# Moving padding columns between the two halves' exponentials, and reordering the first four steps of a dilated-attention plus gated-convolution kernel

## Chip, cores and metric

The kernel runs on one core of one Trainium2 chip. The metric is the device time of one execution in microseconds (us): the median of three runs. A separate execution is recorded by the hardware profiler; all durations of single instructions come from that one.

The engines of the core are called as in the profile: PE (matrix multiply), PEld (PE's loading of weights, which runs beside its matmuls), DVE (vector engine), ACT (scalar engine), POOL (GpSimd) and SP (the engine that here issues most of the transfers). Each engine works through its own instructions in order.

## What is computed

Windowed attention over 8 batches, 8 heads, 576 positions and head width 64, and then a gated unit over the joined heads (width 512). Heads 0 to 3 ("plain") look at the last 32 positions, heads 4 to 7 ("dilated") at every fourth of the last 128.

```python
scores = scale * np.matmul(q, k.transpose(0, 1, 3, 2))
rel = pos[:, None] - pos[None, :]
mask_plain = (rel >= 0) & (rel < window)                       # window 32, heads 0..3
mask_dil = (rel >= 0) & (rel < window * dilation) & (rel % dilation == 0)   # heads 4..7
attn = softmax(where(mask, scores, -1e9));  x = attn @ v       # heads joined: 512 wide
for k in range(K): gate_pre += conv_w[k] * xp[:, k:k + S, :]   # causal, K = 5
gate = 1 / (1 + exp(-gate_pre))
out = (gate * (x @ w_val)) @ w_out
```

All inputs and the output are float32; the kernel computes in bfloat16 with float32 sums.

## The kernel before

**Steps, groups, halves.** The work on attention is cut into 32 steps (`NP`). Step i takes one batch b = i // 4 and a pair of heads c = i % 4; pairs 0 and 1 are plain, 2 and 3 dilated. Two steps make a group g (four heads of one kind), and loads and transposes are made for groups. Inside a step there are two halves, hf = 0 and 1. For each half:

- `scores` (L383) makes six small matmuls into a PSUM tile `ps_sc`; ACT takes the exponential of them (L407) into a half of the tile `et`.
- `apply_mask` (L410) multiplies that half of `et` with a mask of zeros and ones on DVE (L416).
- `attn_v` (L418) makes six matmuls (L434) with 128 columns of `et` as weights and v as the moving operand, which carries a column of ones, so that the row sums come out too.
- `normalize` (L439) takes the reciprocals (L447) and multiplies (L452), on DVE, into `xn`.

One step later `trans_x` (L456) transposes the result into `xT`. The other half of the work is then `conv` (L485), the gate's convolution as six matmuls with diagonal weights `conv_diag` (L503, gate on ACT at L511), `val` (L514, four matmuls and a product on DVE at L524) and `out_tile` (L530, four matmuls, a copy on ACT at L538 and stores).

**Layout of et.** For plain heads (block width `HB` = 288) the weights of attn_v begin at 96 n in the block of one head (n = 0, 1, 2), for dilated ones at 128 n; the load always takes 128 columns, more than a block has left at n = 2. The four blocks of a step lie side by side, first half then second, with 96 columns of ones behind the last:

```python
ets = [consts.tile([128, 4 * HB + 96], BF16, name=f"et{i}") for i in range(NET)]
e3 = et[:, 2 * hf * HB:2 * (hf + 1) * HB].rearrange("p (h n) -> p h n", h=2)
lhsT=et[:, (2 * hf + sl) * HB + col:(2 * hf + sl) * HB + col + 128],
```

Rows of the product that belong to no position are not read.

**Order.** The schedule is written by hand: every engine's instructions stand in the order in which the Python code issues them, and semaphores between the engines are put in by the framework. Transfers are issued on three queues: SP's (most loads and all stores), ACT's (four loads at the beginning) and POOL's (the two weights `w_val` and `w_out`, cast on the way). `load_main` (L110) loads k or q of two or four heads (L115), `load_rest` (L119) the last positions, `load_v` (L138) v, and `load_group` (L164) all of a group. Groups 0 and 1 are loaded in two parts of two heads, group 2 and later ones whole; group g + 3 is issued at the first step of group g.

`cast` (L171) turns k or q of plain groups into bfloat16: for group 0 on DVE and ACT, for later ones on POOL. `trans_main` (L314) and `trans_rest` (L355) transpose k and q of the next group, with copies on ACT and DVE. `make_conv_diag` (L300) builds the five diagonals of one 128-wide block; block c is built at step c on POOL. `warm` (L568) issues matmuls on a tile of ones whose result nobody reads. `pop_conv` (L564) takes the next conv of a list when its due time, i or i + 0.5, is less than the number given.

Of the kernel before, what the change touches and what calls it, by code (L numbers as in the profile page):

```python
# [23 lines left out]
def kernel(  # L24
# [60 lines left out]
    NET = 2  # L85
    ets = [consts.tile([128, 4 * HB + 96], BF16, name=f"et{i}") for i in range(NET)]
    NVP = 2
# [49 lines left out]

    def load_v(g, a=0, e=4):  # L138
        b, dil = g // 2, g % 2
        t = grp_tiles.setdefault(g, {})  # L140
        if not dil:

            dst = vPs[b % NVP].rearrange("p h n e -> p (h n) e")
            first = a * NB
            if b == 0 and a == 0:
                nc.sync.dma_start(out=dst[32:128, 0, 0:D], in_=v[0, 0, 0:96, :])
                first = 1
            nc.sync.dma_start(
                out=dst[:, first:e * NB, 0:D],
                in_=bass.AP(  # L150
                    tensor=v.tensor, offset=v.offset + (b * H * S + 96 * first - 32) * D,
                    ap=[[D, 128], [96 * D, e * NB - first], [1, D]]))
        else:
            if "vst" not in t:
                t["vst"] = vst_pool.tile([128, 4, DIL * D], FP32, name="v_st")
                t["vBst"] = vst_pool.tile([128, 4, 2, D], FP32, name="vB_st")
            nc.sync.dma_start(
                out=t["vst"][:, a:e, :],
                in_=v[b, 4 + a:4 + e, 0:RM, :].rearrange("h (p r) d -> p h (r d)", r=DIL))
            nc.sync.dma_start(  # L160
                out=t["vBst"][:, a:e].rearrange("p h j d -> p h (j d)"),
                in_=v[b, 4 + a:4 + e, DIL * TB:S, :].rearrange("h (p j) d -> p h (j d)", j=2))
# [39 lines left out]
    load_rest(0, "q", nc.scalar)  # L202
    load_v(0, 0, 2)
    load_main(0, "k", 2, 4, nc.sync)
    load_main(0, "q", 2, 4, nc.scalar)
    load_v(0, 2, 4)
    nc.scalar.dma_start(out=conv_nat, in_=moe_conv_w)
    for a in (0, 2):
# [5 lines left out]
        load_v(1, a, a + 2)  # L214
    load_group(2)
    nc.vector.memset(junk, 1.0)  # L216
# [9 lines left out]
    for et in ets:  # L226
        nc.vector.memset(et[:, 4 * HB:], 1.0)
    for i in range(NVP):
# [71 lines left out]
    def make_conv_diag(c):  # L300
        nc.gpsimd.tensor_tensor(  # L301
            out=conv_diag[:, c, :, :],
# [3 lines left out]

    def load_weights():
        for (dst, src) in ((w_val_b, moe_w_val), (w_out_b, moe_w_out)):
            nc.gpsimd.dma_start(out=dst, in_=src.rearrange("(c p) n -> p c n", p=128))

# [72 lines left out]
    def scores(i, hf):  # L383
# [21 lines left out]
        et = ets[i % NET]  # L405
        e3 = et[:, 2 * hf * HB:2 * (hf + 1) * HB].rearrange("p (h n) -> p h n", h=2)
        nc.scalar.activation(out=e3, in_=ps[:, :, 0:HB], func=AF.Exp, scale=scale)  # L407
        st[(i, "et")] = et

    def apply_mask(i, hf):  # L410
        b, c, dil, g, a = pair_info(i)
        et = st[(i, "et")]
        e3 = et[:, 2 * hf * HB:2 * (hf + 1) * HB].rearrange("p (h n) -> p h n", h=2)
        m = mask_d if dil else mask_p[:, 3 * hf:3 * hf + 3, :].rearrange("p n q -> p (n q)")
# [3 lines left out]
    def attn_v(i, hf):  # L418
        b, c, dil, g, a = pair_info(i)
        et, ps = st[(i, "et")], st[(i, hf)]  # L420
        for n in range(3):
            for sl in range(2):
# [3 lines left out]
                else:  # L426
# [8 lines left out]
                    out=ps[:, 0, x * AVS:x * AVS + D + 1],  # L435
                    lhsT=et[:, (2 * hf + sl) * HB + col:(2 * hf + sl) * HB + col + 128],
                    rhs=rhs, start=True, stop=True)
# [139 lines left out]
    trans_rest(0)  # L577
    cast(0, "k", 2, nc.vector)
    cast(0, "q", 2, nc.scalar)
    setup_conv_w()  # L580
    for i in range(NP):
        b, c, dil, g, a = pair_info(i)
        if c % 2 == 0 and g + 3 < 2 * B:
            load_group(g + 3)
        if i + 1 < NP:
            prep_v(i + 1)
        if i == 0:
            make_mask_d()
            make_perm()
        g2 = g + 2  # L590
        if g2 < 2 * B and g2 % 2 == 0:
            cast(g2, "k" if a == 0 else "q", 0, nc.gpsimd)
            cast(g2, "k" if a == 0 else "q", 2, nc.gpsimd)
        if i < NCH:
            make_conv_diag(i)
        if i == 1:
            load_weights()
        scores(i, 0)
        scores(i, 1)
        if i > 0:  # L600
            trans_x(i - 1)
            for G in range(2):
                convs.append((i + 0.5 * G, (b - (c == 0), (c - 1) % NCH, G)))
            if c == 0:
                vals.extend((b - 1, cc, G) for G in range(2) for cc in range(NCH))
        if i == 0:
            trans_main(0, "k", (1,))
# [6 lines left out]
        elif i == 3:  # L614
            trans_main(2, "k")
            trans_main(2, "q")
        elif g + 1 < 2 * B:
            trans_main(g + 1, "k" if a == 0 else "q")
        apply_mask(i, 0)
        if i < 3:  # L620
            warm(2)
        if vals:
            run_val()
        pop_conv(i)
        apply_mask(i, 1)
        if i < 3:
            warm(2)
        attn_v(i, 0)
        normalize(i, 0)
        pop_conv(i + 0.5)  # L630
        if i < 3:
            warm(2)
        attn_v(i, 1)
        normalize(i, 1)
        if i == 3:
            trans_rest(2)
        elif i > 3 and a == 0 and g + 1 < 2 * B:
            trans_rest(g + 1)
        if i < 3:
            warm(3)  # L640
        if outs:
# [47 lines left out]
```

## Time and profile before

| | us |
|---|---|
| median of 3 runs | 200.55 (200.37 to 200.99) |
| the profiled execution, its own time | 202.34 |
| its span, first to last instruction | 200.6 |
| PE busy | 176.8 (88%) |
| DVE busy | 129.3 (64%) |
| ACT busy | 118.9 (59%) |
| POOL busy | 45.0 (22%) |
| granted clock of PE, mean | 0.977 |
| moved by transfers | 42.29 MB, 211 GB/s |

How to read it: busy time is the time in which an engine executes; the rest of the span it waits or has nothing to do. The page also cuts the span into 40 slices of about 5 us and gives each engine's busy tenths; PEclk is the clock granted to PE, in tenths. A list of waits gives, for an engine and line, who released it, the us in total, the number of times and the longest. A matmul's end is modelled, and matmuls overlap, so PE's busy time is not a measure of work done at full speed. Line numbers are those of the kernel before.

The four k and q transposes of group 0's first pair end at about 6 us; scores of steps 0, 1, 2, 3 and 4 begin at 6.93, 14.63, 26.00, 33.03 and 36.72 us. From there a step takes 4 to 6 us, depending on how many output tiles it has.

### The profile page before, as it was taken

How to read it: one execution, taken by the hardware profiler on the slowest of the kernel's cores; microseconds unless marked ns; L12 is line 12 of the kernel's file. 1: busy time of each engine (PE TensorE's matmuls, PEld its weight loads, DVE VectorE, ACT ScalarE, POOL GpSimd, SP SyncE). 2: the span in 40 equal slices, each digit the busy share in tenths (PEclk: the TensorE clock that was granted, in tenths of full speed). 3: DMA queues.
4: the chain of work that ended last, by engine and by line, in shares of the span. 5: the costliest groups of instructions: out<-in, count | busy, mean ns of one | idle time of the engine just before them, and what ended most of it. 6: DMA issues, size and time to landing. Idle time of an engine off the chain costs nothing.

```text
span 200.6 us, 5261 instructions
## 1 busy us (share of the span) xinstructions
PE 176.8 (88%) x2046; PEld 124.9 (62%) x2071; DVE 129.3 (64%) x342; ACT 118.9 (59%) x211; POOL 45.0 (22%) x91
## 2 busy tenths in 40 slices
PE   6595598889899999999899999998999999989990
PEld 2452355767667776777577776776677767665650
DVE  3254066787757875877767776777677767774530
ACT  3514054866757765776577658666676757654331
POOL 7200991160440080000900350007104000000000
PEclk9999579999999999999999999999999999999997
DMA  6989999999959993779969975969595222111334
GB/s 171 271 249 323 192 323 204 294 242 367 301 152 275 360 267 86 253 252 268 227 168 356 332 147 142 346 209 286 157 279 187 56 76 78 62 52 56 106 105 157
DMA packets 62499, 42.29 MB, mean 211 GB/s; under 512 B 31237, under 2 KB 57861, under 8 KB 62474
## 3 DMA queue, kind: packets, MB, share of 16 engines
q1 hardware_dynamic: 60592, 40.31, 72.0%
q0 software_dynamic: 1056, 1.05, 3.3%
q10 hardware_dynamic: 826, 0.60, 1.0%
q8 instruction: 16, 0.26, 0.5%
q14 instruction: 9, 0.07, 0.1%
HBM read 33.56 MB, written 9.44 MB: 214 GB/s over the span
## 4 chain that ended last, share of the span: by engine, by line
PE 65%; DVE 19%; DMA 5%; SPq 4%; issue 2%; POOL 1%; ACT 0%; ACTq 0%
PE ps_bank L533 15%; PE ps_bank L518 13%; PE ps_bank L503 11%; DVE et L416 9%; DVE y_all L524 6%; PE ps_sc L434 6%; PE ps_sc L404 6%; PE ps_bank L325 5%; DMA k_nat<-in_k_dram 3%; PE ps_bank L464 3%; SPq L115 2%; DMA q_nat<-in_q_dram 2%; DVE xT L479 2%; PE ps_bank L477 2%; PE ps_bank L570 2%
## 5 line engine op out<-in xcount | busy, mean ns | idle before, releaser
L503 PE MATMUL ps_bank<-xT,conv_diag 128*128 128x288 bf16 (+1 forms) x384 | 50.8, 268 | 4.5 <-POOL conv_diag L301 4.5
L511 ACT ACTIVATE gate<-ps_bank 128x288 bf16<-128x288 f32 x64 | 26.5, 417 | 32.2 <-PE ps_bank L503 31.1
L407 ACT ACTIVATE et<-ps_sc 128x576 bf16<-128x576 f32 x64 | 38.2, 649 | 12.0 <-PE ps_sc L404 10.5
L518 PE MATMUL ps_bank<-xT,w_val_b 128*128 128x288 bf16 x256 | 41.5, 286 | 0.2 <-DVE xT L479 0.2
L524 DVE SCALAR_TENSOR_TENSOR y_all<-gate,ps_bank 128x288 bf16<-128x288 bf16 x64 | 28.9, 452 | 16.0 <-PE ps_bank L518 13.7
L503 PEld LDWEIGHTS <-conv_diag 128*128 128x128 bf16 x384 | 32.2, 98 | 10.8 <-POOL conv_diag L301 4.6
L538 ACT ACTIVATE osb<-ps_bank 128x512 f32<-128x512 f32 x36 | 21.5, 597 | 27.1 <-PE ps_bank L533 26.8
L452 DVE TENSOR_TENSOR xn<-ps_sc,rec 96x384 bf16<-96x384 f32 (+1 forms) x64 | 35.5, 555 | 2.2
L533 PE MATMUL ps_bank<-w_out_b,y_all 128*128 128x512 bf16 x120 | 35.4, 380 | 1.3
L434 PEld LDWEIGHTS <-et 128*128 128x128 bf16 x384 | 22.8, 99 | 16.5 <-DVE et L416 12.2
L181 POOL CAST k_b<-k_nat 128x512 bf16<-128x512 f32 x14 | 8.7, 650 | 96.9 <-DMA k_nat<-in_k_dram 69.8
L518 PEld LDWEIGHTS <-w_val_b 128*128 128x128 bf16 x256 | 23.5, 98 | 9.5 <-issue 0.4
L479 DVE COPY xT<-ps_bank 128x576 bf16<-128x576 bf16 x32 | 14.6, 458 | 20.2 <-PE ps_bank L477 13.7
L447 DVE RECIPROCAL rec<-ps_sc 96x6 f32<-96x6 f32 (+1 forms) x64 | 12.4, 194 | 18.4 <-PE ps_sc L434 17.6
L533 PEld LDWEIGHTS <-y_all 128*128 128x128 bf16 x144 | 12.7, 97 | 12.0 <-DVE y_all L524 3.7
L416 DVE TENSOR_TENSOR et<-et,mask_d 128x576 bf16<-128x576 bf16 x32 | 19.2, 604 | 0.0
L434 PE MATMUL ps_sc<-vP,et 128*128 128x65 bf16 x192 | 14.2, 200 | 2.6 <-DVE et L416 0.6
L570 PE MATMUL ps_bank<-junk 128*128 128x512 bf16 x34 | 13.4, 513 | 1.6 <-DVE junk L216 1.5
L416 DVE TENSOR_TENSOR et<-et,mask_p 128x576 bf16<-128x576 bf16 x32 | 14.7, 465 | 0.0
L434 PE MATMUL ps_sc<-vB,et 128*128 128x65 bf16 x64 | 9.7, 195 | 5.4 <-DVE et L416 4.4
L188 POOL CAST vA<-v_st 128x512 bf16<-128x512 f32 x16 | 10.7, 668 | 11.7 <-DMA v_st<-in_v_dram 11.7
L340 ACT COPY kT<-ps_bank 128x1024 bf16<-128x1024 bf16 (+1 forms) x9 | 8.3, 919 | 2.4 <-PE ps_bank L325 2.1
(78 smaller groups left out, 191.1 us busy)
## 6 DMA issues: line engine op xcount, KB each, us to landing
k_nat<-in_k_dram SPq DMA_DIRECT2D x14, 512.0 KB, 5.8
q_nat<-in_q_dram SPq DMA_DIRECT2D x14, 512.0 KB, 6.0
vP<-in_v_dram SPq DMA_DIRECT2D x7, 768.0 KB, 8.1
v_st<-in_v_dram SPq DMA_DIRECT2D x7, 512.0 KB, 5.6
out_dram<-osb SPq DMA_DIRECT2D x8, 256.0 KB, 2.6
vB_st<-in_v_dram SPq DMA_DIRECT2D x7, 256.0 KB, 5.8
out_dram<-osb SPq DMA_DIRECT2D x8, 224.0 KB, 2.5
out_dram<-osb SPq DMA_DIRECT2D x8, 192.0 KB, 2.3
```

The costliest lines, as they stand in the source:

```text
L407: nc.scalar.activation(out=e3, in_=ps[:, :, 0:HB], func=AF.Exp, scale=scale)
L416: nc.vector.tensor_tensor(out=e3, in0=e3, in1=m, op=ALU.mult)
L434: nc.tensor.matmul(out=ps[:, 0, x * AVS:x * AVS + D + 1], lhsT=et[:, (2 * hf + sl) * HB + col:(2 * hf + sl) * HB + col + 128], rhs=rhs, st ...
L452: nc.vector.tensor_tensor(out=dst, in0=av[:, :, 0:D], in1=rec[0:R, :, None].to_broadcast([R, 6, D]), op=ALU.mult)
L479: nc.vector.tensor_copy(xTs[b % NXT][:, c, :, 2:], pr)
L503: nc.tensor.matmul(out=ps[:, o * T:(o + n) * T], lhsT=conv_diag[:, c, K - 1 - m, :], rhs=xt[:, c, r:r + n, off:off + T], start=(idx == 0), ...
L511: nc.scalar.activation(out=gate, in_=ps[:, 0:HB], func=AF.Tanh, scale=0.5)
L518: nc.tensor.matmul(out=ps[:, 0:HB], lhsT=w_val_b[:, mc, c * 128:(c + 1) * 128], rhs=xt[:, mc, 2 * G:2 * G + 2, 2:], start=(mc == 0), stop= ...
L524: nc.vector.scalar_tensor_tensor(out=y_all[:, c, b * S + G * HB:b * S + (G + 1) * HB], in0=gates.pop((b, c, G)), scalar=1.0, in1=ps[:, 0:H ...
L533: nc.tensor.matmul(out=ps, lhsT=y_all[:, c, 128 * n:128 * n + 128], rhs=w_out_b[:, c, :], start=(c == 0), stop=(c == NCH - 1),)
L538: nc.scalar.mul(out=osb, in_=ps, mul=0.5)
L570: nc.tensor.matmul(out=bank(), lhsT=junk[:, 0:128], rhs=junk, start=True, stop=True)
```

## The change

It has two parts.

1. The tile `et` becomes three-dimensional, one row of 576 + 96 columns for each half, with the 96 columns of ones behind each half instead of behind both. Writers and readers address their half by its index.
2. The beginning is put into another order. v's first part and conv_w move to ACT's queue, q's second half to SP's; group 2 is loaded in two parts. `make_conv_diag` moves from POOL to DVE and to other places: block 0 before the loop, block c + 1 at the end of step c. The second halves of group 0's k and q are both cast on ACT, behind the exponentials of step 0. The transposes for the next group in steps 0 to 4 move from the middle of the step to its end. POOL loads w_val at step 1 and w_out at step 3, and casts k and q of group 2 at step 2, behind the preparation of v. In steps 0 to 3 the warm matmuls are 3, 1 and 1 inside a step (3 more at the end of steps 0 to 2), where they were 2, 2 and 2 in steps 0 to 2; and the due times given to `pop_conv` are a quarter later, so that step 1 runs two convs.

```diff
--- before.py
+++ after.py
@@ -83,7 +83,7 @@
     NKT = 2
     kTs = [consts.tile([128, 2, KOFF + S], BF16, name=f"kT{i}") for i in range(NKT)]
     NET = 2
-    ets = [consts.tile([128, 4 * HB + 96], BF16, name=f"et{i}") for i in range(NET)]
+    ets = [consts.tile([128, 2, 2 * HB + 96], BF16, name=f"et{i}") for i in range(NET)]
     NVP = 2
     vPs = [consts.tile([128, 4, NB, VS], FP32, name=f"vP{i}") for i in range(NVP)]
     NVD = 2
@@ -135,7 +135,7 @@
                     tensor=src.tensor, offset=src.offset + ((b * H + 4) * S + RM) * D,
                     ap=[[DIL * D, TR], [S * D, 4], [1, DIL * D]]))
 
-    def load_v(g, a=0, e=4):
+    def load_v(g, a=0, e=4, eng=nc.sync):
         b, dil = g // 2, g % 2
         t = grp_tiles.setdefault(g, {})
         if not dil:
@@ -143,9 +143,9 @@
             dst = vPs[b % NVP].rearrange("p h n e -> p (h n) e")
             first = a * NB
             if b == 0 and a == 0:
-                nc.sync.dma_start(out=dst[32:128, 0, 0:D], in_=v[0, 0, 0:96, :])
+                eng.dma_start(out=dst[32:128, 0, 0:D], in_=v[0, 0, 0:96, :])
                 first = 1
-            nc.sync.dma_start(
+            eng.dma_start(
                 out=dst[:, first:e * NB, 0:D],
                 in_=bass.AP(
                     tensor=v.tensor, offset=v.offset + (b * H * S + 96 * first - 32) * D,
@@ -154,10 +154,10 @@
             if "vst" not in t:
                 t["vst"] = vst_pool.tile([128, 4, DIL * D], FP32, name="v_st")
                 t["vBst"] = vst_pool.tile([128, 4, 2, D], FP32, name="vB_st")
-            nc.sync.dma_start(
+            eng.dma_start(
                 out=t["vst"][:, a:e, :],
                 in_=v[b, 4 + a:4 + e, 0:RM, :].rearrange("h (p r) d -> p h (r d)", r=DIL))
-            nc.sync.dma_start(
+            eng.dma_start(
                 out=t["vBst"][:, a:e].rearrange("p h j d -> p h (j d)"),
                 in_=v[b, 4 + a:4 + e, DIL * TB:S, :].rearrange("h (p j) d -> p h (j d)", j=2))
 
@@ -200,11 +200,11 @@
     load_main(0, "q", 0, 2, nc.scalar)
     load_rest(0, "k", nc.sync)
     load_rest(0, "q", nc.scalar)
-    load_v(0, 0, 2)
+    nc.scalar.dma_start(out=conv_nat, in_=moe_conv_w)
+    load_v(0, 0, 2, nc.scalar)
     load_main(0, "k", 2, 4, nc.sync)
-    load_main(0, "q", 2, 4, nc.scalar)
+    load_main(0, "q", 2, 4, nc.sync)
     load_v(0, 2, 4)
-    nc.scalar.dma_start(out=conv_nat, in_=moe_conv_w)
     for a in (0, 2):
         load_main(1, "k", a, a + 2, nc.sync)
         load_main(1, "q", a, a + 2, nc.sync)
@@ -212,7 +212,13 @@
             load_rest(1, "k", nc.sync)
             load_rest(1, "q", nc.sync)
         load_v(1, a, a + 2)
-    load_group(2)
+    for a in (0, 2):
+        load_main(2, "k", a, a + 2, nc.sync)
+        load_main(2, "q", a, a + 2, nc.sync)
+        if a == 0:
+            load_rest(2, "k", nc.sync)
+            load_rest(2, "q", nc.sync)
+        load_v(2, a, a + 2)
     nc.vector.memset(junk, 1.0)
 
 
@@ -224,7 +230,7 @@
     for kt in kTs:
         nc.vector.memset(kt[:, :, 0:KOFF], 0.0)
     for et in ets:
-        nc.vector.memset(et[:, 4 * HB:], 1.0)
+        nc.vector.memset(et[:, :, 2 * HB:], 1.0)
     for i in range(NVP):
         nc.vector.memset(vPs[i][:, :, :, D:D + 1], 1.0 - 2.0 ** -9)
         if i == 0:
@@ -298,15 +304,14 @@
             out=conv_w_sb, in_=ps[:, 0:NCH * 8].rearrange("p (c e) -> p c e", c=NCH)[:, :, 0:K])
 
     def make_conv_diag(c):
-        nc.gpsimd.tensor_tensor(
+        nc.vector.tensor_tensor(
             out=conv_diag[:, c, :, :],
             in0=ident[:, None, :].to_broadcast([128, K, 128]),
             in1=conv_w_sb[:, c, :, None].to_broadcast([128, K, 128]),
             op=ALU.mult)
 
-    def load_weights():
-        for (dst, src) in ((w_val_b, moe_w_val), (w_out_b, moe_w_out)):
-            nc.gpsimd.dma_start(out=dst, in_=src.rearrange("(c p) n -> p c n", p=128))
+    def load_weight(dst, src):
+        nc.gpsimd.dma_start(out=dst, in_=src.rearrange("(c p) n -> p c n", p=128))
 
 
     st = {}
@@ -403,14 +408,14 @@
                     rhs = t["qB"][p0:p0 + D, a + hf, :, :]
                 nc.tensor.matmul(out=o, lhsT=lhsT, rhs=rhs, start=True, stop=True)
         et = ets[i % NET]
-        e3 = et[:, 2 * hf * HB:2 * (hf + 1) * HB].rearrange("p (h n) -> p h n", h=2)
+        e3 = et[:, hf, 0:2 * HB].rearrange("p (h n) -> p h n", h=2)
         nc.scalar.activation(out=e3, in_=ps[:, :, 0:HB], func=AF.Exp, scale=scale)
         st[(i, "et")] = et
 
     def apply_mask(i, hf):
         b, c, dil, g, a = pair_info(i)
         et = st[(i, "et")]
-        e3 = et[:, 2 * hf * HB:2 * (hf + 1) * HB].rearrange("p (h n) -> p h n", h=2)
+        e3 = et[:, hf, 0:2 * HB].rearrange("p (h n) -> p h n", h=2)
         m = mask_d if dil else mask_p[:, 3 * hf:3 * hf + 3, :].rearrange("p n q -> p (n q)")
         m = m[:, None, :].to_broadcast([128, 2, HB])
         nc.vector.tensor_tensor(out=e3, in0=e3, in1=m, op=ALU.mult)
@@ -433,7 +438,7 @@
                 x = 3 * sl + n if dil else 2 * n + sl
                 nc.tensor.matmul(
                     out=ps[:, 0, x * AVS:x * AVS + D + 1],
-                    lhsT=et[:, (2 * hf + sl) * HB + col:(2 * hf + sl) * HB + col + 128],
+                    lhsT=et[:, hf, sl * HB + col:sl * HB + col + 128],
                     rhs=rhs, start=True, stop=True)
 
     def normalize(i, hf):
@@ -575,34 +580,58 @@
     trans_main(0, "k", (0,))
     trans_main(0, "q", (0,))
     trans_rest(0)
-    cast(0, "k", 2, nc.vector)
-    cast(0, "q", 2, nc.scalar)
     setup_conv_w()
+    make_conv_diag(0)
     for i in range(NP):
         b, c, dil, g, a = pair_info(i)
         if c % 2 == 0 and g + 3 < 2 * B:
             load_group(g + 3)
-        if i + 1 < NP:
-            prep_v(i + 1)
         if i == 0:
             make_mask_d()
             make_perm()
+        if i + 1 < NP:
+            prep_v(i + 1)
+        if i == 1:
+            load_weight(w_val_b, moe_w_val)
+        if i == 3:
+            load_weight(w_out_b, moe_w_out)
+        if i == 2:
+            for name in ("k", "q"):
+                cast(2, name, 0, nc.gpsimd)
+                cast(2, name, 2, nc.gpsimd)
         g2 = g + 2
-        if g2 < 2 * B and g2 % 2 == 0:
+        if 2 < g2 < 2 * B and g2 % 2 == 0:
             cast(g2, "k" if a == 0 else "q", 0, nc.gpsimd)
             cast(g2, "k" if a == 0 else "q", 2, nc.gpsimd)
-        if i < NCH:
-            make_conv_diag(i)
-        if i == 1:
-            load_weights()
         scores(i, 0)
         scores(i, 1)
+        if i == 0:
+            cast(0, "q", 2, nc.scalar)
+            cast(0, "k", 2, nc.scalar)
         if i > 0:
             trans_x(i - 1)
             for G in range(2):
                 convs.append((i + 0.5 * G, (b - (c == 0), (c - 1) % NCH, G)))
             if c == 0:
                 vals.extend((b - 1, cc, G) for G in range(2) for cc in range(NCH))
+        if i > 4 and g + 1 < 2 * B:
+            trans_main(g + 1, "k" if a == 0 else "q")
+        apply_mask(i, 0)
+        if i < 4:
+            warm(3)
+        if vals:
+            run_val()
+        pop_conv(i if i > 3 else i + 0.25)
+        apply_mask(i, 1)
+        if i < 4:
+            warm(1)
+        attn_v(i, 0)
+        normalize(i, 0)
+        pop_conv(i + 0.5 if i > 3 else i + 0.75)
+        if i < 4:
+            warm(1)
+        attn_v(i, 1)
+        normalize(i, 1)
         if i == 0:
             trans_main(0, "k", (1,))
             trans_main(0, "q", (1,))
@@ -614,29 +643,14 @@
         elif i == 3:
             trans_main(2, "k")
             trans_main(2, "q")
-        elif g + 1 < 2 * B:
-            trans_main(g + 1, "k" if a == 0 else "q")
-        apply_mask(i, 0)
-        if i < 3:
-            warm(2)
-        if vals:
-            run_val()
-        pop_conv(i)
-        apply_mask(i, 1)
-        if i < 3:
-            warm(2)
-        attn_v(i, 0)
-        normalize(i, 0)
-        pop_conv(i + 0.5)
-        if i < 3:
-            warm(2)
-        attn_v(i, 1)
-        normalize(i, 1)
-        if i == 3:
             trans_rest(2)
-        elif i > 3 and a == 0 and g + 1 < 2 * B:
+        elif i == 4:
+            trans_main(3, "k")
+            trans_rest(3)
+        elif a == 0 and g + 1 < 2 * B:
             trans_rest(g + 1)
         if i < 3:
+            make_conv_diag(i + 1)
             warm(3)
         if outs:
             out_tile(outs.pop(0))
```

## Prediction

> **What bounds the kernel now.** I read the page's slices first: PE is busy 88% of the span, and its row has one hole, in slices 4 and 5 (20 to 30 us), where the granted clock falls too. Then the waits (us in total, times, longest), of which these two end on PE.
>
> ```profile
> PE   6595598889899999999899999998999999989990
> ...
> PEclk9999579999999999999999999999999999999997
> ```
>
> ```profile
> PEld L434 <- DVE et L416: 12.2, 31, 1.2
> ...
> PE ps_bank L503 <- POOL conv_diag L301: 4.5, 1, 4.5
> ```
>
> Two things stand out: one wait of 4.5 us, and one small wait that recurs in nearly every one of the 32 steps. The timeline shows the first. Columns are start and length in us, engine, line.
>
> ```profile
> 9.30 0.43 DVE L181 CAST k_b<-k_nat 128x512 bf16<-128x512 f32 x1 [2.48 <-DMA k_nat<-in_k_dram]
> 11.20 0.82 DVE L416 TENSOR_TENSOR et<-et,mask_p 128x576 bf16<-128x576 bf16 x2
> 14.63 0.58 PE L404 MATMUL ps_sc<-qT,kT 64*128 64x96 bf16 x12
> 19.78 1.17 POOL L181 CAST k_b<-k_nat 128x512 bf16<-128x512 f32 x2 [13.55 <-DMA k_nat<-in_k_dram]
> 20.91 1.26 POOL L301 TENSOR_TENSOR conv_diag<-ident,conv_w_sb 128x640 bf16<-128x640 bf16 x1
> 22.23 1.38 PE L503 MATMUL ps_bank<-xT,conv_diag 128*128 128x288 bf16 x6 [4.52 <-POOL conv_diag L301]
> 27.67 3.27 DVE L416 TENSOR_TENSOR et<-et,mask_d 128x576 bf16<-128x576 bf16 x2
> ```
>
> Exponentials of step 0 end at 8.58, but their masks start at 11.20: in DVE's order the cast of k's second half stands ahead and waits for its load. POOL's first conv_diag stands behind a cast of group 2's k, landed at 19.7; so PE's first conv, in step 1, starts 4.5 us late. In step 2 two masks last 3.27 us beside POOL's conv_diag products.
>
> A steady step:
>
> ```profile
> 91.15 0.32 PEld L434 LDWEIGHTS <-et 128*128 128x128 bf16 x5
> 91.23 0.45 DVE L416 TENSOR_TENSOR et<-et,mask_d 128x576 bf16<-128x576 bf16 x1
> 91.73 0.10 PEld L434 LDWEIGHTS <-et 128*128 128x128 bf16 x1 [0.27 <-DVE et L416]
> 91.75 0.50 PEld L503 LDWEIGHTS <-conv_diag 128*128 128x128 bf16 x6
> 91.98 0.20 DVE L447 RECIPROCAL rec<-ps_sc 128x6 f32<-128x6 f32 x1 [0.30 <-PE ps_sc L434]
> ```
>
> Five of attn_v(i,0)'s six loads go through; the sixth waits for the second mask, the next conv stands behind it, and DVE then idles 0.30 until the sixth matmul is done. Both engines lose it.
>
> **The columns.** A load takes 128 columns. The sixth begins at 288+192=480 (plain heads) or 288+256=544 (dilated), so it crosses 576 into the other half. In the new tile a half is 672 wide: 608 and 672 stay inside. The wait must go; cost: one memset over twice the columns, beside the first loads.
>
> What it is worth: over 48 to 190 us the waits put 9.1 us (26 times) on PEld for L434, but only 3.3 us (7 times) on PE. [...] By PE's row the sum would be 3.3, by PEld's 9.1. I take PEld: the conv's load follows at once at 91.75. What is late next? rec then needs mask1, done at 91.68, and the sixth matmul, which would be done at about 91.7: DVE gains some 0.25 where it is the chain (steps whose scores wait for xn). In about 6 steps a POOL cast stretches the mask (0.66 wait at 97.25); there a val and y_all stand behind PE, DVE idles 0.57 before y_all, and about 0.6 is kept. 20 x 0.25 + 6 x 0.6 = 8.6 us.
>
> **The start: issues.** ACT's queue issues five loads instead of four: q's second half (0.61) goes to SP; v's 24 and 352 KB (0.83 and 0.43) come. [...] Behind it on ACT stand the table load (1.28) and q's cast (0.62), and all of step 0 waits for that: 4.75+0.45+1.28+0.62=7.1 against 5.37 now, 1.75 late. [...] I take 1.75. v lands at 4.75+4.8=9.6, before its use at 10.9. SP gets k, q and v's second halves earlier, and three more issues for group 2 (8 loads instead of 5, 0.5 each), hidden: SP waits 6.3 us for room at 16.99 anyway.
>
> **conv_diag on DVE.** No DVE row shows it. Bounds: the mask's row scaled, 465 x 640/576 = 0.52; the xn row, f32 input, 555 x 640/384 = 0.93. conv_w_sb is f32, so I take 0.8. One stands ahead of step 0's masks, on the path; the three others come at a step's end, before an xT copy that is only due 1.0 us into the next step: hidden; without that cover 0.8 each.
> [...] But the four casts of group 2 (0.61 each) now stand at i=2, beside masks, where now they ran beside an idle DVE. [...] I take two: 0.4 in step 2, 0.4 in step 3.
>
> **Steps 0 to 3.** Step 0: from cast end to exp is 2.02 now, so exps run 9.1 to 10.3; conv_w_sb is there at 9.05, conv_diag(0) to 9.85, three small mask_d operations (0.6) to 10.45, masks to 11.3, attn_v from 10.95 (now about 12), second normalize to 13.2. ACT casts the second halves of q and k behind the exps (2 x 0.62, to 11.55), in time. Transposes of the second pair follow attn_v, now uncovered: to 13.4, qT's copy to 13.9, warm matmuls: scores(1) at 14.3, against 14.63.
> Step 1, from its scores: trans_x at 0.51, xT copy 0.99 to 1.45, masks to 2.3, attn_v(0) 2.35, conv 0.65 and a warm matmul 0.2, attn_v(1) to 3.9. Then the moved transposes, first results 4.35, and ACT's kA, kB, qA (16.06 to 17.36 now: 1.30): 5.7. Now these copies lie beside masks. scores(2) at 20.0, against 26.00.
> Step 2: the same and 0.4: scores(3) at 26.1, against 33.02. Step 3: k's 8 transposes to 4.6, kT and qT copies 1.01+1.02: 6.65 and 0.4, against 3.70: scores(4) at 33.2, against 36.72. Gain 3.5.
> Five warm matmuls more in step 3 (0.21 each) fill waits. A conv more runs in step 1 and one fewer in step 4 (the new due times). Step 4: 5.53 now; without its 0.70 mask wait and one conv (0.65), and with DVE's chain at about 4.3: 4.4. Gain 1.1.
> Loads: w_val's issue moves from 25.34 to about 15, since POOL only waits for v_st (landed 13.3), and w_out's to behind group 2's casts. Group 2's q landed at 22.1; w_val's 1 MB of source at about 270 GB/s pushes it by up to 4 us to 26. The casts are due at 30, so this is hidden, by 4 us.
>
> Sum: 3.5 + 1.1 + 8.6 = 13.2 us. The profiled execution took 202.34 (span 200.6 and 1.7 around it): 189.1 for such a one. The median is 1.8 lower: 200.55 - 13.2 = **187.3**.
>
> **Rivals.**
> Late group 2: w_val's bytes, now ahead, and the casts behind prep_v(3) on POOL make step 4 wait. scores(4) can't come before the last landing + 0.6 cast + 0.5 transposes + 2.0 copies + 0.2. For: DMA's slices stand at 8 or 9 from 5 us on. Against: 4 us of slack. At a landing of 33.4 the start gains nothing: 190.8.
> The wait moves: second-half mask, y_all or xn take its place, and only PE's 3.3 us is kept. For: scores already wait for xn, qB, qT in 18 steps. Against: DVE's own 0.30 idle goes too (7.8 us in all). 187.3 + 5.3 = 192.6.
> Slower: the clock stays at half. In the trace matmuls ran at half speed first, whatever PEclk says (four transposes took 0.61 us at 9.79, 0.39 at 15.41); after PE had idled from 17.7 the granted clock was 0.58 in 20 to 25 us and 0.74 in 25 to 30. Now each step ends with 1 to 2 us of waiting for ACT's copies. At half clock a step's PE work grows by about 3.3 us (a conv 1.38 against 0.78, a warm matmul 0.43 against 0.21). Through steps 1 to 4 that eats the 13.2; with one more step it is 204. Against: warm matmuls fill the ends, and no idle is near the 4.5 us of before.
> That the layout fails to part the halves is excluded by the addresses.
>
> **Numbers.** Forecast 0.73 (187.3; its own range 184 to 190: 1.2 less if ACT does not wait, up to 9.4 from the columns; 2 or 3 more if copies or casts cost more), late loads 0.14, moved wait 0.08, clock 0.05. What this kernel's measurement tells from no change is about 0.3%, 0.6 us. Faster: 0.94; within: 0.01; slower: 0.05. Range 183.5 to 192.5: it takes in the late loads and leaves out the moved wait's end and the clock.
>
> **What would show it.** Right: PEld L434 <- DVE et all but gone; no wait of L503 for conv_diag, whose row stands under DVE at about 0.8; clock full from about 14 us on; the ACT table load near 5.2; scores(4) near 33; rec's wait for PE near nothing. Wrong: scores(4) after 36, POOL's k_b cast later than 30, L404 or y_all waits grown by what L434 lost, PEclk below 9 after slice 3.

## The result, and the profile after

| | before | after |
|---|---|---|
| median, us | 200.46 (4 runs) | 187.5 (186.38 to 188.45, 4 runs) |
| ratio after / before | | 0.9347, 95% interval 0.9292 to 0.9403 |
| the profiled execution, us (its span) | 202.34 (200.6) | 186.38 (184.7) |

The forecast was 187.3. The same kernel measured once more (c1 below) gave 185.46 (ratio 0.9258, 0.921 to 0.9306): single executions of it ran from 184.2 to 188.5 us. Medians here are over all executions; ratios and intervals leave out those that took over 1.5% more than the fastest of their kernel. The profiled execution of before took 1.9 us more than the median, so a second trace of that kernel (f1 below) is compared too.

The rows of PE and of its clock, after:

```profile
PE   6659986999999999999999999999999999999990
PEclk9987999699999999999999999999999999999998
```

The hole of 15 to 25 us is gone. (It is the fourth and fifth digit of PE's row; the prediction puts it at 20 to 30 us, which is where the clock fell.) PE now dips in the seventh digit, 28 to 32 us, where the end of step 3 waits for copies of k and q. The clock still falls, to 0.7 in the fourth digit (14 to 18 us) and 0.6 in the eighth (32 to 37 us). Three of the waits in the first 48 us:

```profile
PE ps_sc L439 <- DMA vP<-in_v_dram: 1.8, 1, 1.8
PEld L439 <- DVE et L421: 1.7, 2, 1.0
PE ps_sc L409 <- ACT qT L342: 1.5, 1, 1.5
```

In the body, before (48 to 190 us) and after (45 to 180 us):

```profile
PEld L434 <- DVE et L416: 9.1, 26, 0.8
DVE rec L447 <- PE ps_sc L434: 7.8, 26, 0.3
PEld L533 <- DVE y_all L524: 3.2, 8, 0.5
```

```profile
PEld L538 <- DVE y_all L529: 3.7, 9, 0.5
PEld L409 <- issue: 2.3, 10, 0.2
PEld L439 <- DVE et L421: 0.4, 2, 0.2
```

In the body PEld waited 9.1 us for `et` before and waits 0.4 now, and rec's wait of 7.8 us for PE is gone. Nothing else on PE took their place: from scores(5) to scores(31) the wait for y_all is 2.4 us in both traces. PE's wait of 4.5 us for conv_diag is gone too; at the start PE now waits 1.8 us for v and 1.5 us for a copy of q.

The start in the timeline:

```profile
4.70 0.39 ACTq L148 DMA_DIRECT2D vP<-in_v_dram  x1
5.13 1.28 ACT L179 ACT_TABLE_LOAD   x1 [5.13 <-DMA q_nat<-in_q_dram]
8.26 0.83 DVE L307 TENSOR_TENSOR conv_diag<-ident,conv_w_sb 128x640 bf16<-128x640 bf16 x1
9.51 0.82 DVE L421 TENSOR_TENSOR et<-et,mask_p 128x576 bf16<-128x576 bf16 x2
11.99 0.32 PE L439 MATMUL ps_sc<-vP,et 128*128 128x65 bf16 x5 [1.77 <-DMA vP<-in_v_dram]
26.59 0.62 POOL L181 CAST k_b<-k_nat 128x512 bf16<-128x512 f32 x1 [7.07 <-DMA k_nat<-in_k_dram]
26.85 1.44 DVE L421 TENSOR_TENSOR et<-et,mask_d 128x576 bf16<-128x576 bf16 x2
31.68 0.43 PE L409 MATMUL ps_sc<-qT,kT 64*128 64x96 bf16 x12 [1.46 <-ACT qT L342]
```

v is issued at 4.70 and reaches PE at 11.99, so most of step 0's attn_v waits for the load and not for its masks. The two masks of step 3 meet POOL's casts: 1.44 us instead of 0.82. And a steady step:

```profile
39.21 0.34 PEld L439 LDWEIGHTS <-et 128*128 128x128 bf16 x6
39.28 0.45 DVE L421 TENSOR_TENSOR et<-et,mask_p 128x576 bf16<-128x576 bf16 x1
39.48 0.50 PEld L508 LDWEIGHTS <-conv_diag 128*128 128x128 bf16 x6
39.71 0.19 DVE L452 RECIPROCAL rec<-ps_sc 96x6 f32<-96x6 f32 x1
```

All six loads go at once while the second mask is still running. From the first of them to the conv's first load it is 39.48 - 39.21 = 0.27 us; before it was 91.75 - 91.15 = 0.60. rec follows the mask with no idle time.

### The profile page after: what moved, and what is told of

It reads as the page before. It is cut to its first block, busy times and chain, and to the rows that moved or that the text cites. A ratio compares the mean times of both kernels' runs of the same rounds, so it can differ in the third digit from the quotient of the medians.

```text
span 184.7 us, 5269 instructions
## 1 busy us (share of the span) xinstructions
PE 170.0 (92%) x2046; PEld 122.2 (66%) x2073; DVE 127.5 (69%) x345; ACT 118.9 (64%) x212; POOL 40.5 (22%) x87
## 4 chain that ended last, share of the span: by engine, by line
PE 85%; DMA 6%; DVE 2%; ACT 2%; issue 2%; ACTq 0%
PE ps_bank L508 22%; PE ps_bank L538 17%; PE ps_bank L523 16%; PE ps_bank L330 7%; PE ps_sc L439 7%; PE ps_sc L409 6%; DMA vP<-in_v_dram 4%; PE ps_bank L469 3%; PE ps_bank L575 3%; DMA q_nat<-in_q_dram 2%; PE ps_bank L482 2%; PE ps_bank L476 2%; DVE xn L457 1%; PE ps_bank L365 1%; ACT qT L342 1%
## 5 line engine op out<-in xcount | busy, mean ns | idle before, releaser
L439 PEld LDWEIGHTS <-et 128*128 128x128 bf16 x384 | 20.4, 98 | 7.4 <-DVE et L421 2.1
L421 DVE TENSOR_TENSOR et<-et,mask_p 128x576 bf16<-128x576 bf16 x32 | 15.9, 501 | 0.0
L421 DVE TENSOR_TENSOR et<-et,mask_d 128x576 bf16<-128x576 bf16 x32 | 15.0, 474 | 0.0
L575 PE MATMUL ps_bank<-junk 128*128 128x512 bf16 x34 | 12.8, 472 | 1.7 <-DVE junk L222 1.5
L439 PE MATMUL ps_sc<-vP,et 128*128 128x65 bf16 x192 | 11.8, 197 | 2.4 <-DMA vP<-in_v_dram 1.8
L181 POOL CAST q_b<-q_nat 128x512 bf16<-128x512 f32 x14 | 9.6, 711 | 0.6 <-DMA q_nat<-in_q_dram 0.6
```

The costliest lines, as they stand in the source:

```text
L181: eng.tensor_copy(dst, src)
L421: nc.vector.tensor_tensor(out=e3, in0=e3, in1=m, op=ALU.mult)
L439: nc.tensor.matmul(out=ps[:, 0, x * AVS:x * AVS + D + 1], lhsT=et[:, hf, sl * HB + col:sl * HB + col + 128], rhs=rhs, start=True, stop=True)
L575: nc.tensor.matmul(out=bank(), lhsT=junk[:, 0:128], rhs=junk, start=True, stop=True)
```

## The experiments

Start of the scores of some steps in each profiled execution (us), the length of steps 3, 4 and 6 there, and the median and ratio of the kernel:

| kernel | scores 1 | 2 | 4 | 7 | 31 | step 3 | step 4 | step 6 | median | ratio |
|---|---|---|---|---|---|---|---|---|---|---|
| before | 14.63 | 26.00 | 36.72 | 51.93 | 178.30 | 3.69 | 5.53 | 5.38 | 200.46 | 1 |
| before, again (f1) | 15.14 | 24.81 | 35.07 | 50.30 | 175.75 | 3.69 | 5.09 | 5.39 | 199.81 | |
| after | 14.52 | 20.40 | 31.68 | 45.98 | 162.87 | 6.10 | 5.46 | 5.06 | 187.50 | 0.9347 |
| after, again (c1) | 14.72 | 19.90 | 31.18 | 44.17 | 161.01 | 6.10 | 3.95 | 5.27 | 185.46 | 0.9258 |
| columns alone (e1) | 14.81 | 24.30 | 33.25 | 47.27 | 164.39 | 3.84 | 4.77 | 5.22 | 188.33 | 0.942 |
| order alone (e2) | 15.24 | 20.43 | 32.07 | 46.46 | 171.93 | 6.45 | 4.60 | 5.62 | 196.01 | 0.9773 |
| conv_w on POOL's queue (e3) | 11.22 | 16.40 | 28.37 | 43.90 | 160.75 | 6.78 | 5.05 | 6.70 | 184.42 | 0.9188 |
| warm matmuls in step 3 (e4) | 15.50 | 20.69 | 32.45 | 45.23 | 163.26 | 6.57 | 3.94 | 5.07 | 186.43 | 0.9316 |
| transposes in mid-step (c2) | 13.64 | 18.85 | 30.00 | 44.35 | 161.07 | 6.30 | 3.94 | 6.63 | 185.87 | 0.9268 |
| conv_diag on POOL (c3) | 17.40 | 23.05 | 34.49 | 47.27 | 164.02 | 6.17 | 3.94 | 5.07 | 189.79 | 0.9462 |
| e3 + e4 + c2 (c4) | 11.44 | 17.00 | 29.55 | 46.64 | 163.74 | 7.71 | 3.94 | 9.37 | 185.87 | 0.9225 |
| c2 + k load earlier (f2) | 15.60 | 21.22 | 32.37 | 45.16 | 162.70 | 6.31 | 3.94 | 5.07 | 184.61 | 0.9209 |
| e3 + k load earlier (f3) | 11.59 | 16.77 | 28.18 | 42.61 | 161.44 | 6.23 | 5.32 | 5.27 | 183.90 | 0.9174 |
| e3 + c2 + k load earlier (f4) | 11.34 | 17.10 | 28.65 | 42.66 | 159.35 | 6.72 | 5.00 | 5.24 | 184.15 | 0.9176 |

**The columns alone, e1.** The kernel before with the new tile.

```diff
-    ets = [consts.tile([128, 4 * HB + 96], BF16, ...
+    ets = [consts.tile([128, 2, 2 * HB + 96], BF16, ...
-                    lhsT=et[:, (2 * hf + sl) * HB + col:(2 * hf + sl) * HB + col + 128],
+                    lhsT=et[:, hf, sl * HB + col:sl * HB + col + 128],
```

> The kernel before with the new tile et alone; no step is reordered. Theory A (the recurring wait of PE's weight loads is lost time on PE and DVE alike, in every step): 10 to 11.5 us faster than before, near 189.5, since the two traces differ by 10.3 us from scores(5) to scores(31), about 0.32 a step where PEld showed 0.26. The prediction's own term would give 8.6 plus about 1 for the early steps, near 191. Rival B (most of the gain is the start's, and the steady steps gain only what PE's own row showed, 3.3 us): near 197.

Measured: 11.9 us less (0.9373 to 0.9467), theory A and 0.4 us more. Three lines of its trace:

```profile
20.85 1.05 PE L503 MATMUL ps_bank<-xT,conv_diag 128*128 128x288 bf16 x6 [2.97 <-POOL conv_diag L301]
25.64 2.77 DVE L416 TENSOR_TENSOR et<-et,mask_d 128x576 bf16<-128x576 bf16 x2
27.05 0.29 PE L434 MATMUL ps_sc<-vA,et 128*128 128x65 bf16 x4
```

The start still waits for POOL's conv_diag, and the two masks of step 2 still take 2.77 us beside POOL's products. But attn_v's first half no longer needs the second of them: it starts at 27.05, and step 2 takes 5.11 us where before it took 6.57 (f1) and 7.03. So the columns earn 9 to 10 us in the body (from scores(5) to scores(31) 126.4 us, against 135.6 in f1 and 136.1 in before) and some 1.5 in step 2.

**The order alone, e2.** The kernel after with the old tile.

> The kernel after with the old tile et (the columns of ones behind both halves); the new order stays. If the parts add up, this gains 13.0 less what the columns alone give: 2 to 3 us by theory A, near 198, although scores(5) began 5.1 us earlier in the trace of after (a part of that is the columns' too, 0.7 in step 4, 1.2 in step 2). Rival B: near 191. In the trace the weight loads should wait again for the second mask, about 26 times after 45 us, and in steps 0 to 3 too, where the new order puts nothing between the masks but one warm matmul.

Measured: 4.2 us less (0.9733 to 0.9814), more than the 2 to 3 of theory A. The body's wait is back:

```profile
PEld L439 <- DVE et L421: 8.0, 25, 0.5
```

Alone the two parts give 11.9 + 4.2 = 16.1; together they gave 13.0 and, in the second measurement (c1), 14.5. The part earned twice is the wait in step 2. In f1's trace of the kernel before it is this:

```profile
26.47 2.83 DVE L416 TENSOR_TENSOR et<-et,mask_d 128x576 bf16<-128x576 bf16 x2
27.73 2.67 POOL L301 TENSOR_TENSOR conv_diag<-ident,conv_w_sb 128x640 bf16<-128x640 bf16 x2
29.35 0.20 PE L434 MATMUL ps_sc<-vB,et 128*128 128x65 bf16 x1 [1.16 <-DVE et L416]
```

The new order takes away what stretches the masks (two take 0.82 us in step 2 of e2); the columns take away the need to wait for the second. Step 2, 6.57 us in f1, takes 5.11 in e1, 5.19 in e2 and 5.18 with both, so 1.4 us are counted twice. That leaves 14.7, near the 14.5 of the second measurement; what the first lacks against it stays open. Of the new order's own edits only those that follow were tried apart: what the place of the casts, of the weight loads and of group 2's loads is worth each is not shown.

**The issue of v, e3.** conv_w's load goes to POOL's queue, so v's large part has one load fewer ahead of it on the other two.

```diff
-    nc.scalar.dma_start(out=conv_nat, in_=moe_conv_w)
...
+    nc.gpsimd.dma_start(out=conv_nat, in_=moe_conv_w)
```

> The kernel after, with conv_w's 10 KB loaded on POOL's queue instead of ACT's, so that v's 352 KB is no longer the ninth load on the two other queues. Theory: ACT no longer waits for q's landing before it issues v; the table load starts near 4.0 instead of 5.13, q's cast ends near 5.9 instead of 7.04, v is issued near 3.5 and lands near 9 to 10 instead of 12.0, so that attn_v(0,0) hardly waits (1.8 us before): scores(1) near 12.5 instead of 14.5, and 1 to 2 us off the total, 185.5 to 186.5. Rival (transfers bound the start, so that work done earlier waits at group 2 instead): no change of the total, scores(4) still near 31.7.

```profile
2.71 0.45 ACTq L148 DMA_DIRECT2D vP<-in_v_dram  x1
3.19 1.28 ACT L179 ACT_TABLE_LOAD   x1 [3.19 <-issue]
9.00 0.32 PE L440 MATMUL ps_sc<-vP,et 128*128 128x65 bf16 x5 [0.17 <-DMA vP<-in_v_dram]
38.55 1.39 POOL L181 CAST k_b<-k_nat 128x512 bf16<-128x512 f32 x2 [11.05 <-DMA k_nat<-in_k_dram]
39.22 0.40 PE L331 MATMUL ps_bank<-ident,k_b 128*128 128x128 bf16 x4 [0.92 <-POOL k_b L181]
```

Measured: 184.42, below the 185.5 to 186.5 expected. In after, v's large part was issued at 4.70, 0.02 us after q's first load had landed. Here it is issued at 2.71 without a wait, the table load starts 1.9 us earlier (3.19 against 5.13) and v's wait shrinks from 1.77 to 0.17: both come with the one load fewer. A part of the lead of 3.3 us at scores(1) is PE's speed in that execution: the three warm matmuls ahead of them took 0.81 us, in after 1.49. scores(4) come about 3 us earlier, but step 6 then waits for the k of group 4, which lands when it lands: 6.70 us instead of 5.06 to 5.27. At scores(7) little of the lead is left (43.90 against 44.17 in c1).

**Warm matmuls in step 3, e4.** Step 4 of the profiled execution ran at a granted clock of 0.84 and 0.82 (30 to 35 and 35 to 40 us); eight more warm matmuls stand in the wait before it.

```diff
+        if i == 3:
+            warm(8)
```

> The kernel after, with eight more warm matmuls at the end of step 3, where PE idles about 1.5 us for the copies of kT and qT. Theory (that idle makes the clock fall to half from 33.3 to 36.8 us in the trace, which ate step 4's gain: 5.46 us where the prediction had 4.4): the granted clock stays full in 30 to 40 us, step 4 takes about 4.5 us, and the total falls by about 1 us. Rival (the fall comes from the whole window's load, not from this idle, or the eight matmuls take as long as they save): no gain, or 0.5 us slower.

Measured: step 4 takes 3.94 us, and step 3, at whose end the matmuls stand, 6.57 instead of 6.10. 186.43 (0.9272 to 0.9361) lies between the two measurements of the kernel after. The next run explains it.

**The same kernel again, c1.**

> The changed kernel itself, unchanged, as the partner of the three others on this chip. By every theory 187.5 us, ratio 0.935 to the kernel before. What it can still tell: whether the stretch at half clock in step 4 (slices near 33 to 37 us, step 4 at 5.46 us) belongs to the kernel or to the one execution profiled. If to the kernel, step 4 again takes 5.2 to 5.6 us; if to the execution, 4.0 to 4.4.

```profile
PEclk9859999999999999999999999999999999999998
```

The clock stays at 9 tenths from the fourth digit on, and step 4 took 3.95 us with no warm matmul more. The fall in step 4 belongs to the one execution; e4's step 4 is no effect of its edit that these runs can tell from chance. (e3 and f4 met such a fall in their step 4: PEclk is 6 tenths in e3's seventh slice, 27 to 32 us, and 7 and 8 in f4's seventh and eighth, 27 to 36 us, and the step's first conv took 1.36 and 1.39 us, in c1 0.78; f3's step 4 waited 1.2 us for a load of q.) Why this median is 2 us below the first one stays open.

**Transposes of group 1 in the middle of steps 1 and 2, c2.**

```diff
+        if i in (1, 2):
+            trans_main(1, "k", (i - 1,))
+            trans_main(1, "q", (i - 1,))
+            if i == 1:
+                trans_rest(1)
         apply_mask(i, 0)
```

> The changed kernel with the transposes of group 1's k and q back in the middle of steps 1 and 2 (ahead of the masks), where the kernel before had them. My theory: at the end of the step they cost the wait for ACT's copies, up to 1.3 us in each of the two steps, which in the middle lies beside masks and attn_v; scores(2) and scores(3) come earlier, by 1 to 2 us together, and the time is 185.5 to 186.5. Rival one: the step is bound by DVE's and ACT's chain either way, and nothing changes (187.5). Rival two, for which they would have been moved: group 1's loads land later than the middle of the step, PE stands before the masks and attn_v behind the transposes, and it is slower, 188.5 or more, with PE's transposes waiting for the load of group 1's k or q by over 1 us.

Measured: no difference in time (185.87 against 185.46 on the same chip). scores(4) came 1.2 us earlier, but 1.1 us of that stood at scores(1), ahead of the edit. There c1 was at half speed and this execution was not, as the three warm matmuls at the end of step 0 show, c1's first:

```profile
13.34 1.45 PE L575 MATMUL ps_bank<-junk 128*128 128x512 bf16 x3
```

```profile
12.43 0.81 PE L575 MATMUL ps_bank<-junk 128*128 128x512 bf16 x3
```

Steps 1 to 3 together took 16.36 us, in c1 16.46. So these traces give the edit itself about 0.1 us, which is rival one; the expectation of f2 below still credits it with the 1.2. And step 6 gave the lead back, a thing that no theory had:

```profile
39.00 1.39 POOL L181 CAST k_b<-k_nat 128x512 bf16<-128x512 f32 x2 [10.88 <-DMA k_nat<-in_k_dram]
39.67 0.40 PE L330 MATMUL ps_bank<-ident,k_b 128*128 128x128 bf16 x4 [0.84 <-POOL k_b L181]
```

**conv_diag on POOL at the new places, c3.**

```diff
-        nc.vector.tensor_tensor(
+        nc.gpsimd.tensor_tensor(
             out=conv_diag[:, c, :, :],
```

> The changed kernel with the five-diagonal product back on POOL, at the new places. My theory (by the kernel before's rows: 1.26 us on POOL, two masks 3.27 us beside it): block 0 costs 0.45 us more ahead of step 0's first conv only if that is what PE waits for, and the three later ones take nothing from DVE's chain at a step's end; masks of the next step that meet the product are stretched by up to 1 us each. Sum 187.5 to 189.5, with two masks in steps 1 to 3 at 1.5 to 3 us. Rival: where DVE was the chain in steps 0 to 3, 0.8 us a step comes back and it is faster, 185.5.

Measured: 4.3 us slower than c1, and not mainly by masks. Step 0 takes 9.09 us instead of 6.44:

```profile
8.55 1.26 POOL L307 TENSOR_TENSOR conv_diag<-ident,conv_w_sb 128x640 bf16<-128x640 bf16 x1 [5.04 <-ACT conv_w_sb L303]
11.78 0.17 DVE L290 TENSOR_SCALAR par_i<-par_i 128x2 int32<-128x2 int32 x1 [3.19 <-POOL par_i L289]
12.21 1.41 DVE L293 TENSOR_TENSOR mask_d<-mask_d,same 128x32 bf16<-128x32 bf16 x1
12.32 1.25 POOL L307 TENSOR_TENSOR conv_diag<-ident,conv_w_sb 128x640 bf16<-128x640 bf16 x1
14.04 0.51 PE L439 MATMUL ps_sc<-vP,et 128*128 128x65 bf16 x6 [3.24 <-DVE et L421]
```

POOL waits 5.04 us for conv_w, and everything behind it on POOL waits too: the pieces of mask_d, among them par_i, for which DVE stands 3.19 us ahead of step 0's masks. The last piece on DVE, a product of only 128x32, takes 1.41 us while POOL runs its own product; in after it took 0.19. Steps 1 to 3 are longer by 0.47, 0.09 and 0.07 us only. A place behind mask_d's pieces on POOL was not tried.

**All three start edits together, c4.**

> The changed kernel with three edits together: conv_w's load on POOL's queue (3 us faster alone), eight warm matmuls at the end of step 3 (0.6 to 1 faster alone) and group 1's transposes in the middle of steps 1 and 2. If the gains add up: 184.4 less 0.8 less what the transposes give, 182 to 183.6. Rival, by what the load edit alone showed (step 6 took 6.7 us and waited for group 4's k): loads bound there, whatever is gained before it is given back at step 6, and the time is 184 to 185 with step 6 at 7.5 us or more.

Measured: 185.87 (0.9159 to 0.929), not to be told from c1. In the profiled execution scores(4) came 1.6 us earlier, but k_b's cast started at 40.02 after 12.23 us of waiting for its load, and step 6 took 9.37 us. This is the rival's mechanism: what is gained before is given back there. But the execution traced took 187.37 us and the fastest of the six 182.97, so the 9.37 us are no measure of the median's loss.

**The kernel before again, f1.** One execution, 199.81 us.

> The kernel before itself, one look, to see in which steps the profiled execution of before (202.34 us) lost its 1.8 us against the median. If it was the clock around the hole at 20 to 27 us: here step 1 takes 10 to 10.6 us instead of 11.37 and step 2 5.5 to 6.5 instead of 7.03, scores(4) begin near 35, and every step from 5 on takes what it took there within 0.05 us. If the loss lay all along the span: scores(4) near 36.7 again, and later steps shorter by some 0.05 us each.

The first theory held for the start, not for the later steps. Of the 2.55 us by which scores(31) come earlier than in the first trace, 1.65 lie ahead of scores(4): step 1 took 9.67 and step 2 6.57 us instead of 11.37 and 7.03. Step 1's first conv ran at full rate (0.80 us for six matmuls, 1.38 there). Steps 4 and 5 together took the same in both (9.83 and 9.84), and the other 0.9 lie in some of the steps with a cast on POOL (5.94 and 5.95 us in steps 7 and 15, before 6.36 and 6.35).

**The k of group 4 ahead of group 3's v, f2 to f4.** The same bytes in another order, on c2, on e3 and on both.

```diff
+        if i == 0:
...
+            load_main(4, "k", 0, 4, nc.sync)
+            load_v(3)
```

> The changed kernel with group 1's transposes in the middle of steps 1 and 2, and now group 4's k load issued ahead of group 3's v (768 KB, by 270 GB/s some 2.8 us). Without the second edit scores(4) came 1.2 us earlier than in the changed kernel and step 6 took 6.63 us instead of 5.27, waiting for k_b of group 4. My theory (transfers bound there): k_b's cast starts at 36 to 37.5 instead of 39.0, step 6 takes 5.1, scores(7) begin near 42.9 and the time is 184.2 to 184.8. Rival: the bytes are the same and group 3's v (due at attn_v of step 6) is late instead; then step 6 stays at 6 us or more and the time does not change (185.5 to 186).

> The changed kernel with conv_w's load on POOL's queue and group 4's k load ahead of group 3's v. Without the second edit scores(4) came at 28.37, but steps 4 and 6 took 5.05 and 6.70 and scores(7) stood at 43.90. Theory: step 6 takes 5.1, scores(7) 42.0 to 42.5, time 182.5 to 183.5, the best so far. Rival: v of group 3 or a load of group 5 is late next, scores(7) to scores(9) no earlier than 43.5 to 54, time 184 to 185.

> Both start edits (conv_w on POOL's queue, group 1's transposes in the middle of steps 1 and 2) and group 4's k load ahead of group 3's v. Scores(4) come near 27. If the transfers' order was all that held it back: scores(7) near 41, time 181.5 to 182.5. If the transfers' sum holds it back (by 37 us some 10 MB at 270 GB/s have to come): no better than the one with conv_w alone, within 0.6 us, with a wait for a load of 1 us or more in steps 5 to 8.

f2: step 6 takes 5.07 us and waits for no load, so the load's place in the queue was the cause of c2's wait. From scores(4) to scores(7) it is 12.8 us against 14.35 in c2. The time, 184.61, is as expected, though its interval (0.9155 to 0.9263) overlaps with c2's (0.9228 to 0.9309); scores(7) are not, as in the profiled execution v landed 0.9 us later than in c2 and PE was at half speed up to scores(1) (at 15.60): the three warm matmuls ahead of them took 1.49 us, in c2 0.81. f3: step 6 is 5.27 and scores(7) come at 42.61, 1.6 us before c1's, near what was expected; the time, 183.9, is above the 182.5 to 183.5 expected. The profiled execution lost 1.9 us later, in steps 14, 16 and 24 (5.49, 5.27 and 5.52 us where c1 took 4.76, 4.88 and 4.80). Its waits and two of its lines say why:

```profile
ACT osb L544 <- DMA out_dram<-osb: 8.1, 7, 2.2
```

```profile
78.24 0.60 ACT L544 ACTIVATE osb<-ps_bank 128x512 f32<-128x512 f32 x1 [2.21 <-DMA out_dram<-osb]
78.89 0.65 PE L524 MATMUL ps_bank<-xT,w_val_b 128*128 128x288 bf16 x4 [0.58 <-ACT osb L544]
```

ACT's copy of an output tile waits for an earlier store to free its buffer, and in step 14 PE's next product waits for the copy; steps 16 and 24 hold such waits of ACT of 1.5 and 1.7 us. c1 has this wait once, 0.8 us (both have three more of up to 1 us that the profile puts down to loads). f4: the time, 184.15, is no better than f3's, and scores(4) came no earlier. Neither theory had the reason: in e3, f3 and f4 the first cast of group 2's second k half waits for its load and starts at 25.08, 24.89 and 25.36, and scores(4) follow 3.3 us later in each, whether step 3 begins at 21.6 or 21.95.

e3, f3 and f4 are the fastest kernels here, 184.4, 183.9 and 184.2. Their intervals (0.9146 to 0.923, 0.9126 to 0.9221, 0.9126 to 0.9226) lie below the first one of the change, and overlap a little with the second (0.921 to 0.9306); among themselves they are not told apart.

## Why the prediction was right, step by step

**The sum.** By their own times the first pair of traces differs by 202.34 - 186.38 = 16.0 us, the pair f1 and c1 by 15.3, the medians by 13.0 and 14.5; the sum was 13.2. So the forecast of 187.3 held, with two terms too small. That it met the first median within 0.2 us is chance in part: the second median stands 1.8 us below the forecast, and the terms as measured add up to more than either median shows. By the terms, for the pair f1 and c1, whose difference lies nearer that of the medians (PEclk is 5 tenths in the third slice of both, 10 to 15 us in f1 and 9 to 14 in c1), and for the first pair:

| term | predicted | f1 to c1 | first pair |
|---|---|---|---|
| start, up to scores(4) | 3.5 | 3.9 | 5.0 |
| step 4 | 1.1 | 1.14 | 0.07 |
| steps 5 to 30, scores(5) to scores(31) | 8.6 | 9.7 | 10.3 |
| from scores(31) to the end | in the 8.6 | 0.6 | 0.5 |

**The columns: right in mechanism, the 0.25 us a step too small.** An ordinary step lost 0.32 us (4.09 to 3.77, 5.12 to 4.80, 4.96 to 4.64), not 0.25: 20 x 0.32 = 6.4 instead of 5.0. I had taken the listed wait of 0.27, which counts from the end of the fifth load. But the loads overlap: six of 0.10 us take 0.34 together, so the sixth would have begun before the fifth's end, and what PE lost is 0.60 - 0.27 = 0.33. The steps with a POOL cast, put at 0.6, gave 0.3 to 0.7 between f1 and c1, 0.3 to 0.9 in the first pair. PEld's row (9.1) was a better measure than PE's (3.3); it was still below what went, 9.7 and 10.3. The rival of the moved wait falls: from scores(5) to scores(31) no wait of PE or PEld grew by more than 0.3 us in all.

**The start: near by two errors that cancel.** ACT's queue was held: v's large part was issued at 4.70, q's first load having landed at 4.68 (I had reckoned with an issue at 4.75), the table load came at 5.13 (predicted 5.2), and q's cast ended at 7.04 against 5.37 in before, 1.67 us late (predicted 1.75); e3 shows the price. In the traces of before, after and e3 eight loads of the two queues start by 3.00 without a wait, and the ninth at 4.75, 4.26 and 4.90, when the first k or q has landed. What makes it wait is not shown. conv_diag took 0.83 on DVE (0.8). But conv_w was there sooner: conv_diag at 8.26 instead of 9.05, the masks at 9.51 instead of 10.45. And v, put at 9.6 by the latency of before, came at 11.99. So scores(1) stood at 14.52, predicted 14.3. Steps 1 to 3 were put at 5.7, 6.1 and 7.1 and took 5.88, 5.18 and 6.10 (5.18, 5.18 and 6.10 in c1). Step 2 met no cast. In step 3 two masks did grow from 0.82 to 1.44, but a conv stands between them and attn_v, whose loads went at 27.63 without waiting: the 0.4 that I put on the path was hidden, and no run shows it there. (The columns hide it: in e2, with the old tile, step 3 took 6.45 us.) The 0.4 was my estimate from one mask of 0.89 us beside a cast, at 39.75 in the trace of before, against 0.45 without. What came in step 3 is 1.44 - 0.82 = 0.62 us for its two masks. Beside a POOL product c3's DVE product of 128x32 took 1.41 us, 0.19 without.

**Late loads: the slack was smaller than I had put it.** Group 2's k landed at 26.6 and the last q cast ended at 27.15 + 1.62 = 28.77; PE took it at 29.45. So the cover was 0.7 us, not 4. The landing itself was well placed (26); the 270 GB/s behind it is about the mean of the GB/s row of before from 5 to 50 us, 274; the 4 us left out the casts between it and PE, which took 2.2 us, and step 3 came 0.5 us sooner than I had put it. The rival did not happen here, but it is the next bound: e3, f3 and f4 stand on this landing, c2, c4 and e3 on that of group 4.

**The clock.** I had expected full clock from 14 us on, and had named a fall after slice 3 as a sign of being wrong; it came, and the forecast held all the same. Windows of the first trace show 0.87 in 15 to 20 us and 0.84 and 0.82 in 30 to 40. In that execution it ate the whole gain of step 4 (six conv matmuls took 1.39 us there, 0.78 in c1). In before the fall around 20 to 27 us (0.58 in 20 to 25, 0.74 in 25 to 30) lies in steps 1 and 2, which took 2.2 us more than in f1; how much of that is the clock's is not shown. What decides on a fall these runs do not settle. In the trace of after the clock fell at 33.35 us, to 0.51 over 33.35 to 36.80; PE's longest wait shortly ahead of that was the 1.46 us for the copy of q, up to 31.68. c1 had the same wait of 1.46 us, up to 31.18, and its clock was 1.00 in 30 to 40 us. By that wait alone the fall is not explained.

## What to carry to other kernels

A weight load that reads a few columns too many can wait for a writer of data that nobody uses. Here it was found where PEld, not PE, waits briefly and often (9.1 us in 26 places, PE 3.3 in 7), and its price was read from load to load (0.33 us), not from the listed wait (0.27). At a start that is bound by transfers, an edit that brings the steps forward is worth only what the next landing allows (e3's scores(4) came 2.8 us ahead of c1's, its scores(7) 0.3): list each cast's wait for its load, and move the load that lands last ahead of one that has slack (step 6 took 6.63 us in c2, 5.07 in f2). Two parts of a change that remove the same wait are not to be added (11.9 and 4.2 us alone, 13.0 and 14.5 together).

## What the runs showed of the hardware

Six weight loads of 128x128, 0.10 us each, passed in 0.34 us. The load of v (352 KB) took 7.3 us from issue to use when issued at 4.70, 6.3 when issued at 2.71. A DVE product of 128x32 with two inputs took 1.41 us beside a POOL product and 0.19 without one. In executions with the same step 0 PE ran the three warm matmuls of step 0 in 1.45 us (c1) or in 0.81 (c2), so that the start of one trace is not to be compared with that of another to a microsecond. And ACT's waits for output stores vary: 8.1 us in seven places in f3, 0.8 in one in c1, but 0.7 in one in f4 as well, which has f3's order of loads; their cause was not tested.
